# Turning q and k on VectorE in 32x32 blocks, from the seventh head pair on

## The chip, the core and the metric

The kernel runs on one core of a Trainium2 chip. A core has five engines that run their own instruction streams in order and wait for one another through semaphores: PE (TensorE, the matrix unit; its weight loads are listed apart as PEld), DVE (VectorE), ACT (ScalarE), POOL (GpSimd) and SP (SyncE, which here only issues DMAs). SBUF is the working memory of 128 partitions; PSUM, in eight banks, is where PE writes.

The metric is the device time of one execution in microseconds (us). Before the change the median of three runs is 283.14 us (282.72 to 283.64).

## The reference, cut to what matters

Inputs are q, k, v of shape (batch 4, heads 8, tokens 768, dim 64) in fp32. Each token of q and of k gets a 6-bit bucket: the signs of its six products with the columns of `proj`. A query attends only to the keys of its own bucket:

```
q_bits = einsum(q, proj) > 0          # 6 signs for each token
k_bits = einsum(k, proj) > 0
mask   = bucket(q)[:, None] == bucket(k)[None, :]
attn   = softmax(where(mask, q @ k.T / 8, -1e9))
x      = (attn @ v), heads joined to (4, 768, 512)
x_prev = x shifted by one token
xk, xr = mu * x + (1 - mu) * x_prev    # two mixes
out    = sigmoid(xr @ w_r) * (relu(xk @ w_k) ** 2 @ w_v)
```

## The kernel before

**Pairs and slots.** The eight heads of a batch are handled as four pairs, so there are 16 pairs `n`, and `NPB` is 4. A pair has 12 slots: two heads `j`, each with six chunks `jc` of 128 keys. In a slot, `score` (L319) makes a 128x768 tile of scores on PE with two matmuls, and ACT takes its exponential into `pt` (L332). Two slots later `pv` (L340) multiplies six blocks of `pt` with v and adds them up in a PSUM bank `oo`; after the sixth chunk DVE divides by the sum (L363, L364) into `ob`.

**The mask inside the score.** The operands of the score have 70 rows: 64 of the head's turned q or k, and 6 of plus or minus one half for the bucket bits (tiles `aq`, `ak`, three sets used in turn). Equal buckets give a product larger by enough that after the scaled exponential all other keys vanish.

**Preparing a pair.** This is the part that the change touches. `load_qk` (L227) brings q and k of a pair in with tokens on partitions: partition p holds the six tokens 6p to 6p+5. `turn` (L263) transposes three 128x128 fp32 blocks of one head of one side on PE (L269) into a PSUM bank; DVE copies them to `tq` (L272) or scales them to `tk` (L274); then POOL casts one half to bf16 into `aq` or `ak` (L277) and DVE the other (L278). There are four such calls for each pair. `bits` (L281) multiplies the turned tiles with `proj` (L287), DVE makes plus or minus one half of the signs (`sg`, L291), and eight small DMAs on the SP queue put them under the operands (L297). `norm` (L254) adds up squares on ACT for a check of the range at the end; a pair below `NKEEP` = 6 has its norms only in the tail of the kernel. `values` (L302) casts v on POOL and sums it.

**The second half: mixing and the channel mix.** `turn_out` (L371) transposes `ob` on PE (L378), DVE copies it to `xt` (L379), and POOL (DVE for the last pair of a batch) makes the copy shifted by one token (L384). `mix` (L389) is three steps on DVE: a difference `df` (L394), times mu (L398), plus the shifted tile (L405). The matmuls of the channel mix (L424) are a list of items with costs in us of PE (`ffn_items`, L508), first `k` and `r` items and then `v` items; `ffn` (L524) plays them out twice in each slot, so that the channel mix of one batch fills the slots of the next batch. Results of `k` items go through a relu on ACT (L447) or DVE (L449) and a square on DVE (L455), of `r` items through a tanh on ACT (L464), of `v` items through DVE (L487) to the output DMA (L491).

**What sets the order.** The schedule is written by hand: the loop from L605 on issues everything slot by slot, and each engine runs its own instructions in that order. With s for the slot in pair n: loads of pair n+3 and of v at s = 3 (5 in the first pair); `bits` for n+1 at s = 1 (3 in the first); `turn_out` of n-1 at s = 3; the first mix at s = 4, the second at s = 8; the four turns for n+2 at s = 5, 7, 9, 11; `values` at s = 6 and 10; `norm` for n+1 at s = 8 and 10, from n+1 = 6 on. `later` (L214) postpones an instruction by a number of slots. PSUM banks go by letter: two score tiles, and single banks A to D. From pair 4 on, the outputs of both heads use bank A, turns, bits and `turn_out` use B, and the channel mix C and D. The weights w_v come through two staging tiles (`load_wv`, L542) and are cast by POOL (L550) eight slots after their load is issued.

## Time and profile before

The profiled execution took 281.45 us; its span, from the first to the last instruction, is 279.6 us. It lies 1.69 us below the median of the timed runs.

| | before |
|---|---|
| median of 3 runs | 283.14 us |
| profiled execution, and its span | 281.45 us, 279.6 us |
| PE busy | 262.2 us (94%) |
| ACT busy | 215.0 us (77%) |
| DVE busy | 198.6 us (71%) |
| POOL busy | 113.3 us (41%) |
| DMA moved | 29.95 MB, mean 107 GB/s |
| pairs 0 to 3, without the channel mix | up to about 58.7 us |
| pairs 4 to 15, with it | about 58.7 to 243.5 us |
| channel mix of the last batch alone | about 243.5 us to the end |

In a timeline, a line begins with the start and the duration in us, then the engine, the line of the kernel, the operation, output and inputs with their shapes, and in brackets how long the engine sat idle before it and what ended the wait. The duration of a matmul includes the time that it spends in the pipe beside its neighbours; what it costs in a row of matmuls is the distance from one start to the next.

### The profile page before, as it was taken

To read this page: it belongs to the slowest core of one execution; us is meant where nothing else is said; L and a number is where in the kernel's file an instruction comes from. 1 tells how busy PE (TensorE), PEld (TensorE's weight loads), DVE (VectorE), ACT (ScalarE), POOL (GpSimd) and SP (SyncE) were. 2 spreads that over 40 slices of the span, in tenths; PEclk is the share of its full clock that TensorE was granted. 3 is DMA by queue.
4 is the path that set the end of the run, shared out by engine and by line. 5 is a ranking of instruction groups with operands and counts; after the bars stand their busy time and mean duration, and the time that the engine had idled before them with its cause. 6 is when DMAs were issued, how large, how long until landed. Compare 5 with 4: busy or idle time off the path is not lost.

```text
span 279.6 us, 6894 instructions
## 1 busy us (share of the span) xinstructions
PE 262.2 (94%) x2530; PEld 165.4 (59%) x2561; DVE 198.6 (71%) x438; ACT 215.0 (77%) x318; POOL 113.3 (41%) x300
## 2 busy tenths in 40 slices
PE   7999997899999999999999999999999889989991
PEld 5466765666565665656565765656565556545540
DVE  3766839879997866769698766769698835576541
ACT  2199995898799896878989896878998898449800
POOL 5885667665554350714455260715444600000000
PEclk9999997999999999999999999999999999999997
DMA  7459597253213050726122040815220001320042
GB/s 231 167 115 208 179 328 248 43 173 101 77 59 117 6 172 4 218 110 191 59 69 108 14 164 7 272 53 166 84 60 4 5 2 39 114 76 2 0 151 86
DMA packets 19896, 29.95 MB, mean 107 GB/s; under 512 B 2184, under 2 KB 15056, under 8 KB 19856
## 3 DMA queue, kind: packets, MB, share of 16 engines
q1 hardware_dynamic: 17928, 25.89, 27.9%
q0 software_dynamic: 1536, 3.15, 5.3%
q8 instruction: 22, 0.36, 0.5%
q10 hardware_dynamic: 392, 0.40, 0.5%
q14 instruction: 18, 0.15, 0.2%
HBM read 24.12 MB, written 6.29 MB: 109 GB/s over the span
## 4 chain that ended last, share of the span: by engine, by line
PE 66%; ACT 9%; DVE 8%; DMA 7%; issue 3%; SPq 3%; POOL 2%; ACTq 0%; DVEq 0%
PE sc L325 15%; PE vp L424 13%; PE kp L424 12%; PE oo L352 8%; ACT pt L332 6%; PE rp L424 5%; DMA wvs<-in_moe_w_v_dram 4%; PE bb L287 4%; PE tpq L269 3%; PE tpk L269 2%; SPq L297 2%; PE ot L378 2%; ACT sq L256 2%; PE oo L343 1%; DMA aq<-sg 1%
## 5 line engine op out<-in xcount | busy, mean ns | idle before, releaser
L332 ACT ACTIVATE pt<-sc,expb 128x768 bf16<-128x768 f32 x192 | 166.5, 904 | 39.4 <-PE sc L325 38.1
L325 PE MATMUL sc<-aq,ak 70*128 70x384 bf16 x384 | 94.9, 328 | 3.2 <-ACT pt L332 0.8
L352 PEld LDWEIGHTS <-pt 128*128 128x128 bf16 x1152 | 61.1, 98 | 26.6 <-issue 0.8
L352 PE MATMUL oo<-va,pt 128*128 128x65 bf16 x1152 | 66.9, 194 | 0.0
L424 PE MATMUL kp<-xk,wk_sb 128*128 128x384 bf16 x256 | 57.7, 325 | 0.8 <-DVE os L487 0.8
L325 PEld LDWEIGHTS <-ak 70*128 70x128 bf16 x384 | 34.9, 98 | 29.3 <-issue 9.1
L424 PE MATMUL vp<-wv_sb,k 128*128 128x512 bf16 (+1 forms) x186 | 50.3, 370 | 0.4 <-issue 0.2
L277 POOL CAST aq<-tq 64x384 bf16<-64x384 f32 x32 | 21.1, 658 | 63.3 <-DVE tq L272 63.3
L455 DVE TENSOR_TENSOR k<-kr 128x384 bf16<-128x384 bf16 x64 | 29.0, 459 | 15.5 <-ACT kr L447 14.3
L424 PEld LDWEIGHTS <-wk_sb 128*128 128x128 bf16 x256 | 22.2, 97 | 13.3 <-issue 4.2
L256 ACT ACTIVATE sq<-qk 128x768 bf16<-128x768 f32 x32 | 27.1, 847 | 0.1
L424 PE MATMUL rp<-wr_sb,xr 128*128 128x512 bf16 x79 | 24.9, 379 | 1.2 <-DVE kr L449 0.8
L424 PEld LDWEIGHTS <-k 128*128 128x128 bf16 x200 | 17.5, 97 | 12.0 <-issue 2.7
L447 ACT ACTIVATE kr<-kp 128x384 bf16<-128x384 f32 x36 | 17.7, 491 | 7.4 <-PE kp L424 7.4
L487 DVE SCALAR_TENSOR_TENSOR os<-th,vp 128x512 f32<-128x512 bf16 (+1 forms) x25 | 16.5, 663 | 9.0 <-PE vp L424 8.9
L384 POOL COPY xt<-xt 128x127 bf16<-128x127 bf16 x12 | 3.6, 302 | 46.4 <-DVE xt L379 46.4
L311 POOL TENSOR_TENSOR s<-vf 128x192 f32<-128x192 f32 x32 | 20.8, 650 | 0.0
L277 POOL CAST ak<-tk 64x384 bf16<-64x384 f32 x32 | 19.3, 602 | 2.4 <-DVE tk L274 2.4
L274 DVE TENSOR_SCALAR tk<-tpk 128x384 f32<-128x384 f32 x32 | 17.6, 550 | 3.4 <-PE tpk L269 3.3
L272 DVE COPY tq<-tpq 128x384 f32<-128x384 f32 x32 | 17.7, 552 | 2.1 <-PE tpq L269 2.0
L269 PE MATMUL tpq<-ident,qk 128*128 128x128 f32 x96 | 16.9, 287 | 2.4 <-DVE tq L272 1.7
L379 DVE COPY xt<-ot 128x768 bf16<-128x768 bf16 x16 | 8.9, 558 | 14.3 <-PE ot L378 14.2
(60 smaller groups left out, 320.0 us busy)
## 6 DMA issues: line engine op xcount, KB each, us to landing
vf<-in_v_dram SPq DMA_DIRECT2D x16, 384.0 KB
out_dram<-os SPq DMA_DIRECT2D x23, 256.0 KB
qk<-in_q_dram SPq DMA_DIRECT2D x13, 384.0 KB
qk<-in_k_dram SPq DMA_DIRECT2D x13, 384.0 KB
wvs<-in_moe_w_v_dram SPq DMA_DIRECT2D x4, 512.0 KB
aq<-sg SPq DMA_DIRECT2D x64, 4.5 KB
wk_sb<-in_moe_w_k_dram POOLq DMA_DIRECT2D x2, 512.0 KB, 5.4
ak<-sg SPq DMA_DIRECT2D x62, 4.5 KB
```

The source lines that it names most:

```text
L256: nc.scalar.activation(junk, nats[n][:, i].rearrange("p j f -> p (j f)"), AF.Square, accum_out=nrm[:, i, n : n + 1],)
L269: nc.tensor.transpose(tp[:, cols], nats[n][:, i, j, cols], ident32)
L272: nc.vector.tensor_copy(dst, tp)
L274: nc.vector.tensor_scalar(out=dst, in0=tp, scalar1=ALPHA, scalar2=None, op0=ALU.mult)
L277: nc.gpsimd.tensor_copy(au[side, j][0:D, 0:HALF], dst[0:D, :])
L311: nc.gpsimd.tensor_add(s3, vf[:, 0 : 3 * D], vf[:, 3 * D : 6 * D])
L325: nc.tensor.matmul(sc[:, sp, 0:HALF], au["k", j][:, jc * P : (jc + 1) * P], au["q", j][:, sp * HALF : (sp + 1) * HALF], start=True, stop=True,
L332: nc.scalar.activation(pt.rearrange("p (s q) -> p s q", s=2), sc[:, :, 0:HALF], AF.Exp, bias=expb, scale=SCALE,)
L352: nc.tensor.matmul(oo[:, ic, :], pts[n, j, jc][:, ic * P : (ic + 1) * P], vas[n, j][:, jc, :], start=False, stop=(jc == NC_ - 1 and ic == ...
L424: nc.tensor.matmul(box["t"], lhs(), rhs(), start=(i == 0), stop=(i == len(mms) - 1))
L447: nc.scalar.activation(kr, kp, AF.Relu)
L455: 1, lambda: nc.vector.tensor_tensor(out=k2, in0=kr, in1=kr, op=ALU.mult)
```

## The change

It has four parts.

1. Pairs 6 to 15 are no longer turned on PE. `load_blocks` brings q and k in block rows: for each side and head two DMAs of 32 partitions, one for each half of the 64 dims, with 24 consecutive tokens on a partition. A DMA reads its 6016 bytes of a row in one piece, so the other half of the dims is read along and not used. `turn_blocks` transposes 32x32 blocks on DVE, one instruction for a side of a pair, with both heads in one 128x768 tile; POOL casts the first head to bf16 and DVE the second, one slot later. `bits_blocks` does the projection on these tiles. For these pairs `norm`, `values` and `turn_out` take the matching token order. The loads of pair 5's v and of all from pair 6 on are issued at s = 6 instead of 3; the turns are at s = 6 and 9; `norm` runs one pair earlier.
2. From pair 4 on the second head's output goes to bank B instead of A; `bits` moves from s = 1 to s = 4, `turn_out` from s = 3 to s = 2, and the second mix from s = 8 to s = 7.
3. In pairs 1 to 3 the three steps of the first mix are issued at s = 6, 8 and 10 instead of all at s = 4.
4. The staging of w_v uses the two new block tiles, each for two loads, so that no load waits for a cast, and the cast comes ten slots after the load instead of eight.

```diff
+            blkp = pool("blk", 2)
+            turnp = pool("turn", 1)
-            t32p = pool("t32", 1)
-            stg = pool("stg", 2)
...
+            def load_blocks(n):
+                b, t = divmod(n, NPB)
+                xb = blkp.tile([P, 2, NTOK, D], FP32, name=f"blk{n}", tag="blk")
+                blks[n] = xb
+                run = NTOK * D - 32
+                for side, i, src in SIDES:
+                    for j in range(2):
+                        rows = src[b, 2 * t + j].rearrange("(i u) d -> i (u d)", u=NTOK)
+                        for h in range(2):
+                            r0 = 32 * (2 * j + h)
+                            nc.sync.dma_start(
+                                out=xb[r0 : r0 + 32, i].rearrange("p u d -> p (u d)")[:, 0:run],
+                                in_=rows[:, 32 * h : 32 * h + run],
+                            )
...
+            def turn_blocks(n, i):
+                side = "qk"[i]
+                au = augs[n % NSET]
+                tt = turnp.tile([P, S], FP32, name=f"t{side}{n}", tag=f"t{side}")
+                nc.vector.transpose(
+                    out=tt.rearrange("p (c i u) -> p u c i", c=NC_, u=4),
+                    in_=blks[n][:, i, :, 0:32].rearrange("p (u c) d -> p u c d", u=4),
+                )
+                turned[n, side] = tt
+
+                def cast(eng, j):
+                    src = tt[j * D : (j + 1) * D, :]
+                    dst = au[side, j][0:D, :]
+                    if side == "q":
+                        eng.tensor_copy(dst, src)
+                    else:
+                        eng.tensor_scalar(
+                            out=dst, in0=src, scalar1=ALPHA, scalar2=1.0,
+                            op0=ALU.mult, op1=ALU.mult,
+                        )
+
+                cast(nc.gpsimd, 0)
+                later(1, lambda: cast(nc.vector, 1))
...
-            def mix(b, dc, i):
+            def mix(b, dc, i, steps=(0, 1, 2)):
...
             def load_wv(c0):
-                st = stg.tile([P, 2, DM], FP32, name=f"wvs{c0}", tag="stg")
+                if c0 in (0, 4):
+                    mx["wvs"] = blkp.tile([P, 2, 2, DM], FP32, name=f"wvs{c0}", tag="blk")
+                st = mx["wvs"][:, c0 % 4 // 2]
...
-                    8,
+                    10,
...
-                return "AC"[j] if n < NPB else "A"
+                return "AC"[j] if n < NPB else "AB"[j]
...
-                if live and s == (5 if n == 0 else 3):
+                if live and s == (5 if n == 0 else 3 if n < NPB - 1 else 6):
                     if n + 3 < NPAIRS:
-                        load_qk(n + 3)
+                        (load_qk if n + 3 < NKEEP else load_blocks)(n + 3)
...
-                    if s == (3 if n == 0 else 1) and n + 1 < NPAIRS:
-                        bits(n + 1, (0, 1), mb)
-                    if s == 3 and n >= 1:
+                    if s == (3 if n == 0 else 1 if n < NPB else 4) and n + 1 < NPAIRS:
+                        if n + 1 < NKEEP:
+                            bits(n + 1, (0, 1), mb)
+                        else:
+                            bits_blocks(n + 1, mb)
+                    if s == (3 if n < NPB else 2) and n >= 1:
                         turn_out(n - 1, mb)
-                    if s == 4 and n >= 1:
+                    if s == 4 and n >= NPB:
                         mix((n - 1) // NPB, (n - 1) % NPB, 0)
+                    if s in (6, 8, 10) and 1 <= n < NPB:
+                        mix(0, n - 1, 0, [s // 2 - 3])
...
-                    if n > NPB and s == 8:
+                    if n > NPB and s == 7:
                         mix((n - 1) // NPB, (n - 1) % NPB, 1)
-                    if s in (5, 7, 9, 11) and n + 2 < NPAIRS:
+                    if s in (5, 7, 9, 11) and n + 2 < NKEEP:
                         x = (s - 5) // 2
                         turn(n + 2, x % 2, x // 2, mb)
+                    if s in (6, 9) and NKEEP <= n + 2 < NPAIRS:
+                        turn_blocks(n + 2, s // 9)
...
-                    if s in (8, 10) and NKEEP <= n + 1 < NPAIRS:
-                        norm(n + 1, (s - 8) // 2)
+                    if s in (8, 10) and NKEEP <= n + 2 < NPAIRS:
+                        norm(n + 2, (s - 8) // 2)
```

## The prediction

> **What bounds the kernel now.** I read the page first, then the busy time by pair, then the timelines of single engines inside one pair.
>
> ```profile
> span 279.6 us, 6894 instructions
> PE 262.2 (94%) x2530; PEld 165.4 (59%) x2561; DVE 198.6 (71%) x438; ACT 215.0 (77%) x318; POOL 113.3 (41%) x300
> PE   7999997899999999999999999999999889989991
> ACT  2199995898799896878989896878998898449800
> ```
>
> PE is the busiest engine in every slice, but ACT shows eights and nines beside it for most of the span. The average does not say which of the two would stop a faster PE, so I cut the span from one pair's bits to the next:
>
> ```profile
> core 0: us, PE busy (x) PEld busy (x) DVE busy (x) ACT busy (x) POOL busy (x), PEclk, DMA share, GB/s
> 58.72:73.11 14.39, 13.56 (x152) 9.05 (x149) 12.74 (x30) 13.10 (x20) 8.08 (x21) 1.00 0.47 165
> 104.64:120.05 15.41, 15.25 (x153) 9.48 (x155) 10.93 (x24) 12.17 (x17) 6.23 (x17) 1.00 0.41 133
> 135.93:151.63 15.70, 15.51 (x158) 10.00 (x160) 13.81 (x31) 14.30 (x23) 6.59 (x17) 1.00 0.23 80
> 198.13:213.80 15.67, 15.36 (x161) 9.83 (x167) 13.82 (x30) 14.58 (x24) 6.87 (x20) 1.00 0.10 30
> 213.80:228.76 14.96, 13.29 (x135) 7.81 (x138) 9.21 (x21) 13.00 (x21) 4.31 (x14) 1.00 0.02 4
> ```
>
> The rows are pairs 4, 7, 9, 13 and 14. A full pair takes 15.2 to 15.9 us, and PE is busy for all but 0.2 to 0.3 us of it. There are two kinds. Where the channel mix plays `v` items (pair 7), ACT needs 12.2 us and DVE 10.9: PE alone is the bound. Where it plays `k` and `r` items (pairs 9, 13), ACT is at 14.3 to 14.6 us and DVE at 13.8: three engines are nearly full. Pair 14 has no turns already and still takes 14.96 us with PE busy 13.29.
>
> **1. Turns leave PE (pairs 4 to 13 issue them).** The cost of a turn is read from the starts in pair 7:
>
> ```profile
> 111.78 0.49 PE L325 MATMUL sc<-aq,ak 70*128 70x384 bf16 x2
> 112.10 0.35 PE L352 MATMUL oo<-va,pt 128*128 128x65 bf16 x6
> 112.50 0.49 PE L269 MATMUL tpk<-ident,qk 128*128 128x128 f32 x3
> 112.83 0.38 PE L424 MATMUL vp<-wv_sb,k 128*128 128x512 bf16 x1
> ```
>
> Three transposes hold PE from 112.50 to 112.83, 0.33 us. Four calls a pair make 1.3 us, ten pairs 13 us; that is the most this part can give. The bits stay at four matmuls (0.78 us a pair) and only move. How much of the 1.3 us arrives depends on ACT:
> - Pairs 7, 8, 11, 12 (ACT 12.2 to 12.7 us in the same table): PE stays the bound at 14.1 us and ACT would be 86 to 90% full. I take 1.2 us each, 4.8 us.
> - Pairs 6, 9, 10, 13 (ACT 14.8, 14.3, 14.3, 14.6): PE would need about 14.4 us, as much as ACT. Two engines that wait for each other through two score tiles do not both run full; today ACT reaches 91 to 93% here. At 95% the pairs take 15.6, 15.1, 15.1 and 15.3 us: gains 0.3, 0.6, 0.7, 0.35, together 1.95 us.
> - Pair 5 (15.59 us, ACT 13.3): 0.9 us.
> - Pair 4: its first half has no channel mix, and it now gets two norms (0.83 us each between starts) that pair 5 had; the last two leave pair 14. ACT goes from 13.1 to 14.8 us, more than the pair lasts today: a loss of 0.5 us. Pair 14 loses 1.66 us of ACT work; of its 1.7 us of PE gaps I take back 0.7 us.
>
> Sum: 4.8 + 1.95 + 0.9 - 0.5 + 0.7 = 7.85 us.
>
> **2. What DVE gets instead.** For one pair it loses these (mean ns after the bar):
>
> ```profile
> L272 DVE COPY tq<-tpq 128x384 f32<-128x384 f32 x32 | 17.7, 552 | 2.1 <-PE tpq L269 2.0
> L274 DVE TENSOR_SCALAR tk<-tpk 128x384 f32<-128x384 f32 x32 | 17.6, 550 | 3.4 <-PE tpk L269 3.3
> L278 DVE CAST ak<-tk 64x384 bf16<-64x384 f32 x32 | 15.3, 479 | 1.1
> L278 DVE CAST aq<-tq 64x384 bf16<-64x384 f32 x32 | 12.1, 377 | 1.1
> L277 POOL CAST aq<-tq 64x384 bf16<-64x384 f32 x32 | 21.1, 658 | 63.3 <-DVE tq L272 63.3
> ```
>
> 4 x 0.55 + 2 x 0.48 + 2 x 0.38 = 3.9 us. It gets two 128x768 fp32 turns, which no row shows. Low end: the slope between the 384-element copy (0.55) and the 512-element L487 (0.68) is about 1.05 ns an element, so 0.95 us. High end: each of the 24 blocks pays one smallest DVE instruction (the 0.059 us memset) on top: 2.4 us. The nearest row is the fp32 copy, so I take 1.0 us. The two casts double in size: from 0.38 us, at most 0.75 each. New sum 2 x 1.0 + 2 x 0.75 = 3.5 us, 0.4 less; with 2.4 us a turn it is 6.3 us, 2.4 more. This lies beside PE and ACT and costs nothing while DVE stays under them: 13.8 - 0.4 = 13.4 us of about 15.1 in pair 9. Its cover is gone at the high end (16.2 us), which is a rival below.
>
> [...]
>
> POOL gets two casts of 768 elements (0.8 to 1.0 us by the 128x1024 cast, 1.03 us) for four of 0.6 to 0.66: no change on an engine 6 to 8 us busy a pair. But the order turns round: today DVE and POOL are released together and DVE's cast starts at once; now POOL starts first and DVE comes a slot later. A DVE cast beside a busy POOL took 3.06 us at 46.85, against 0.35 alone. So a cast can be held by 0 to 2.7 us, and the squares and copies behind it on DVE too. POOL's runs around the casts are 1 to 3 us; I expect 0.5 us each, inside DVE's room.
>
> **3. Loads and the SP queue.** Two q and k loads (0.38 to 0.47 us of SP each) become eight, and the bytes double, by about 0.75 MB a pair. An SP issue costs 0.38 us at the least (output) and 0.7 us (bits), so eight cost 3.0 to 5.6 us instead of 0.9. With bits 5.6, v 0.4 and at most four outputs 1.6, SP is busy 10.6 to 13.2 us of 14.2. The bytes add about 0.16 to a DMA share of 0.23 to 0.47 (147 GB/s at 0.45). Blocks are needed 12 slots after their issue, bits 8 slots, some 9 us, against about 5 us of issue and landing. I cost it at nothing; the cover is these slots, and beyond them PE waits for bits or DVE for a block.
>
> **4. Bank B, `turn_out` at s = 2, bits at s = 4, mix at s = 7.** The wait of head 1's first `pv` for bank A was 0.2 us in all, so the bank gives 0 to 0.2 us. The earlier `turn_out` leaves one slot less for the division: PE has 1.14 us of work between the last `pv` and the transposes (three half-slots of channel mix, 0.27 each, and a score, 0.33), and at the end of pair 7 DVE finished `ob` 1.0 us after that `pv` (119.74 to 120.73). With DVE late PE waits: 0 to 0.6 us a pair; 0.1 in eleven pairs is 1.0 us lost. POOL's shifted copy gets a slot more, so DVE's waits of 0.4 us for it go; they are not on the path.
>
> **5. The early stretch.** Here a wait is on the path (lines of four engines):
>
> ```profile
> 36.78 1.04 POOL L550 TENSOR_SCALAR wv_sb<-wvs 128x1024 bf16<-128x1024 f32 x1 [1.79 <-DMA wvs<-in_moe_w_v_dram]
> ...
> 41.23 0.56 DVE L394 TENSOR_TENSOR df<-xt 128x768 bf16<-128x768 bf16 x1 [3.52 <-POOL xt L384]
> ...
> 43.36 0.55 PE L269 MATMUL tpq<-ident,qk 128*128 128x128 f32 x3 [1.75 <-DVE tq L272]
> ...
> 44.33 1.87 ACT L332 ACTIVATE pt<-sc,expb 128x768 bf16<-128x768 f32 x2 [1.86 <-PE sc L325]
> ```
>
> POOL stands on a w_v load, the shifted copy is late, DVE waits 3.52 us in the mix with a turn's copy behind it, then PE and ACT, the bound in pairs 0 to 3, wait. ACT's gaps from 43 to 52 us add up to 3.8 us. With the cast two slots later and the mix two slots behind the copy, this chain should go. Late next are the 0.4 us gaps at each set of bits. Ends 0 and 3.3 us; I take 2.0, since a second cast still meets POOL's descriptor work for w_r.
>
> **Sum.** 7.85 + 2.0 - 1.0 = 8.85 us from 281.45 us is 272.6 us. Since that execution is 1.69 us below the median of the runs, I forecast 274.3 us for the median after.
>
> **Rivals.**
> - *ACT takes the whole place of PE in the `k` pairs.* The 1.95 us goes, pairs 4 and 5 give nothing, the early chain is halved: 4.8 - 0.5 + 0.7 + 1.0 - 1.0 = 5.0 us, 278 us. For it: ACT 14.3 to 14.8 us. Against: PE and ACT idle at different moments today.
> - *All of it arrives.* 13 + 3.3 = 16.3 us, 267 us. Against: pair 14 with no turns needed 14.96 us.
> - *DVE becomes the bound; slower.* If a turn costs 2.4 us and the POOL order holds both casts 1 us each, DVE in pairs 4, 5, 6, 9, 10, 13 needs about 13.4 + 2.8 + 2 = 18.2 us against 15.7: 15 us lost in six pairs, 6.8 won elsewhere: 291 us. It decides from about 16 us of DVE work a pair. Against: the fp32 copies run at 1.05 ns an element, and pair 7 has 4.5 us of DVE to spare.
>
> That the turns don't leave PE is excluded: PE's stream has no L269 block for pairs 6 to 15.
>
> **Chances and range.** Forecast (270 to 277): 0.52. ACT (277 to 282): 0.18. All of it (266 to 270): 0.10. DVE bound or held, above 284: 0.17. Nothing measurable (within 0.3%, what a measurement of this kernel can tell from no change): 0.03. 8 in 10 lie between 268 and 285. Faster 0.79, same 0.04, slower 0.17.
>
> **What the profile after would show.** Right: no PE transposes of q or k after 60 us, pairs 7, 8, 11, 12 at 14.1 to 14.4 us with PE full, pairs 9, 10 near 15 us with ACT above 94%, no DVE wait of 3.5 us for the shifted copy near 41 us, the new turn at about 1 us. Wrong: turns near 2 us or DVE casts held for a microsecond, PE waiting for DVE in `k` pairs, or scores waiting for bits because SP is late. What makes it wrong first is the unseen turn and the order of the two casts.

## The result, and the profile after

The changed kernel takes 293.65 us (median of 4 runs, 292.53 to 294.64), against 283.08 us (282.72 to 283.64) for the kernel before beside it: ratio 1.037, 95% interval 1.0335 to 1.0402. It is 10.6 us slower. The forecast was 274.3 us, with 268 to 285 as its range; the rival that came nearest is the slower one, at 291 us. The profiled execution took 292.92 us, its span is 291.1 us.

Below, each experiment is told by its difference to the kernel before run on the same chip, whose median was 282.0 to 282.5 us there. In three experiments some executions ran at a lower granted clock than the rest (0.954 against 0.970 to 0.982 in one of 4 with the old slots, 0.978 against 0.984 to 0.995 in one of 10 with three places moved, 0.974 to 0.980 against 0.984 to 0.994 in 4 of 10 with the signs' place alone); the ratios leave those out, so a ratio need not be the quotient of the two medians.

The first lines of the page of the kernel after, and its slices of PE and ACT:

```profile
span 291.1 us, 6646 instructions
...
PE 254.1 (87%) x2412; PEld 151.2 (52%) x2441; DVE 211.4 (73%) x398; ACT 215.9 (74%) x318; POOL 111.2 (38%) x280
...
PE   7899999988696989997896979997896999989990
...
ACT  2298887979587797968789777877888888539800
```

PE lost 8.1 us of busy time and 7 points of share; from the eleventh slice on it has slices of six and seven, where before every slice from the eighth to the last but one was eight or nine. No engine is busier than 87%. DVE rose from 198.6 to 211.4 us although it was forecast to fall a little. The busy time by pair, cut from one pair's output transposes to the next; the rows are pairs 7, 9 and 14:

```profile
core 0: us, PE busy (x) PEld busy (x) DVE busy (x) ACT busy (x) POOL busy (x), PEclk, DMA share, GB/s
110.76:125.71 14.95, 14.29 (x141) 7.95 (x142) 11.83 (x20) 12.31 (x17) 6.35 (x17) 1.00 0.58 148
...
143.31:161.22 17.91, 14.73 (x145) 8.64 (x149) 15.15 (x26) 13.57 (x21) 6.12 (x16) 1.00 0.51 120
...
226.36:241.18 14.82, 13.84 (x144) 8.26 (x146) 8.43 (x20) 12.88 (x19) 4.01 (x14) 1.00 0.02 5
```

Pair 7, which plays `v` items, gained 0.5 us; pair 14, with ACT relieved of the norms, 0.3. Pair 9, which plays `k` items, went from about 15.7 to 17.9 us, with PE busy 14.7, ACT 13.6 and DVE 15.2: none is full. What stands between them is shown by DVE's timeline in pair 9, from the sign's threshold on (start, duration, in brackets the idle time before it and what ended it):

```profile
147.18 0.56 DVE L353 TENSOR_SCALAR sg<-bb 128x384 bf16<-128x384 f32 x1 [2.33 <-PE bb L345]
...
150.03 1.57 DVE L319 STREAM_TRANSPOSE tq<-blk 128x768 f32<-128x768 f32 x1
...
151.82 1.66 DVE L329 CAST aq<-tq 64x768 bf16<-64x768 f32 x1
...
155.53 1.59 DVE L319 STREAM_TRANSPOSE tk<-blk 128x768 f32<-128x768 f32 x1
...
157.33 1.62 DVE L331 TENSOR_SCALAR ak<-tk 64x768 bf16<-64x768 f32 x1
...
159.53 0.55 DVE L539 TENSOR_SCALAR kr<-kp 128x384 bf16<-128x384 f32 x1
```

DVE stands idle for 2.33 us on the sign matmuls `bb`, which the change moved to slot 4, and then works without a gap from 147.18 to past 161 us: mix, turn, cast, division, mix, turn, cast. The relu `kr` that PE needs to get its PSUM bank back stands at the end of that row; PE waited 1.27 us for it, until 160.13. Three things show in it: a wait that was not there, a turn of 1.57 us where 1.0 was costed, and casts of 1.6 us. The groups (count, busy us and mean ns after the bar):

```profile
L319 DVE STREAM_TRANSPOSE tk<-blk 128x768 f32<-128x768 f32 x10 | 15.7, 1566 | 0.0
L319 DVE STREAM_TRANSPOSE tq<-blk 128x768 f32<-128x768 f32 x10 | 15.6, 1560 | 0.0
L329 DVE CAST aq<-tq 64x768 bf16<-64x768 f32 x10 | 10.9, 1089 | 0.3
L331 DVE TENSOR_SCALAR ak<-tk 64x768 bf16<-64x768 f32 x10 | 9.6, 961 | 0.3
L545 DVE TENSOR_TENSOR k<-kr 128x384 bf16<-128x384 bf16 x64 | 25.9, 413 | 11.7 <-ACT kr L537 10.9
```

And the waits in pairs 4 to 14 (us in total, times, longest):

```profile
ACT pt L419 <- PE sc L412: 28.9, 38, 3.4
DVE sg L353 <- PE bb L345: 19.6, 10, 2.7
PEld L464 <- DVE ob L451: 9.2, 10, 2.8
PE kp L514 <- DVE kr L539: 9.0, 7, 1.9
PE ot L464 <- DVE ob L451: 5.5, 6, 2.4
PE rp L514 <- DVE kr L539: 3.2, 3, 2.0
```

In the kernel before the same two waits, in pairs 4 to 14, were:

```profile
DVE sg L291 <- PE bb L287: 0.7, 3, 0.2
PE rp L424 <- DVE kr L449: 0.8, 1, 0.8
```

Now PE waits 12.2 us for relus and 5.5 us for the division `ob`, both DVE's, and ACT waits for PE's scores.

### The profile page after: what moved, and what is told of

Same layout as the page of the kernel before. It is cut to its first block, busy times and chain, and to the rows that moved or that the text cites. A ratio compares the mean times of both kernels' runs of the same rounds, so it can differ in the third digit from the quotient of the medians.

```text
span 291.1 us, 6646 instructions
## 1 busy us (share of the span) xinstructions
PE 254.1 (87%) x2412; PEld 151.2 (52%) x2441; DVE 211.4 (73%) x398; ACT 215.9 (74%) x318; POOL 111.2 (38%) x280
## 2 busy tenths in 40 slices
DMA packets 18296, 37.48 MB, mean 129 GB/s; under 512 B 3144, under 2 KB 10896, under 8 KB 18256
## 4 chain that ended last, share of the span: by engine, by line
PE 40%; DVE 34%; DMA 11%; ACT 5%; issue 4%; SPq 3%; POOL 1%; ACTq 0%; DVEq 0%
PE vp L514 9%; PE sc L412 8%; PE kp L514 7%; PE oo L439 4%; PE rp L514 4%; DMA vf<-in_v_dram 4%; DVE tq L319 4%; DVE tk L319 3%; ACT pt L419 3%; DVE aq L329 3%; DVE ob L451 3%; DVE k L545 3%; DMA qk<-in_k_dram 2%; PE bb L345 2%; DVE xk L496 2%
## 5 line engine op out<-in xcount | busy, mean ns | idle before, releaser
L419 ACT ACTIVATE pt<-sc,expb 128x768 bf16<-128x768 f32 x192 | 166.7, 905 | 46.2 <-PE sc L412 44.1
L412 PEld LDWEIGHTS <-ak 70*128 70x128 bf16 x384 | 34.9, 98 | 36.4 <-issue 15.1
L329 POOL CAST aq<-tq 64x768 bf16<-64x768 f32 x10 | 9.8, 980 | 66.7 <-DVE tq L319 53.3
L545 DVE TENSOR_TENSOR k<-kr 128x384 bf16<-128x384 bf16 x64 | 25.9, 413 | 11.7 <-ACT kr L537 10.9
L537 ACT ACTIVATE kr<-kp 128x384 bf16<-128x384 f32 x36 | 17.9, 496 | 9.4 <-PE kp L514 9.4
L514 PEld LDWEIGHTS <-k 128*128 128x128 bf16 x200 | 16.7, 97 | 13.6 <-issue 3.7
L398 POOL TENSOR_TENSOR s<-vf 128x192 f32<-128x192 f32 x32 | 22.5, 704 | 0.0
L353 DVE TENSOR_SCALAR sg<-bb 128x384 bf16<-128x384 f32 x10 | 5.6, 558 | 19.6 <-PE bb L345 19.6
L331 POOL TENSOR_SCALAR ak<-tk 64x768 bf16<-64x768 f32 x10 | 10.4, 1042 | 22.0 <-DVE tk L319 22.0
L451 DVE TENSOR_TENSOR ob<-oo,rc 128x384 bf16<-128x384 f32 x32 | 17.8, 558 | 1.1
L539 DVE TENSOR_SCALAR kr<-kp 128x384 bf16<-128x384 f32 x28 | 15.4, 550 | 2.6 <-PE kp L514 2.5
L287 ACT ACTIVATE sq<-blk 128x768 bf16<-128x768 f32 x20 | 17.0, 849 | 0.0
L319 DVE STREAM_TRANSPOSE tk<-blk 128x768 f32<-128x768 f32 x10 | 15.7, 1566 | 0.0
L319 DVE STREAM_TRANSPOSE tq<-blk 128x768 f32<-128x768 f32 x10 | 15.6, 1560 | 0.0
```

The source lines that it names most:

```text
L287: nc.scalar.activation(junk.rearrange("p (u d) -> p u d", u=NTOK), blks[n][:, i, :, 0:32], AF.Square, scale=1.5, accum_out=nrm[:, i, n : n ...
L319: nc.vector.transpose(out=tt.rearrange("p (c i u) -> p u c i", c=NC_, u=4), in_=blks[n][:, i, :, 0:32].rearrange("p (u c) d -> p u c d", u=4),
L329: eng.tensor_copy(dst, src)
L398: nc.gpsimd.tensor_add(s3, vf[:, 0 : 3 * D], vf[:, 3 * D : 6 * D])
L412: nc.tensor.matmul(sc[:, sp, 0:HALF], au["k", j][:, jc * P : (jc + 1) * P], au["q", j][:, sp * HALF : (sp + 1) * HALF], start=True, stop=True,
L419: nc.scalar.activation(pt.rearrange("p (s q) -> p s q", s=2), sc[:, :, 0:HALF], AF.Exp, bias=expb, scale=SCALE,)
```

## The experiments

The rows below are the times in us from one pair's first output transpose to the next, read from PE's timeline of each profiled execution. A kernel that issues the output transposes at slot 2 shows the last slot in pair 15, so its sum is about 1.5 us longer for that alone.

```
pair                         4     5     6     7     8     9    10    11    12    13    14    15   sum
before                    15.6  15.5  15.8  15.5  16.0  15.6  15.7  15.5  15.3  15.5  15.1  11.2  182.3
after                     17.1  19.3  15.8  14.9  17.6  17.9  16.7  14.9  17.0  16.5  14.8  12.7  195.3
dense turn                16.7  15.9  15.4  14.3  16.7  16.7  16.1  14.4  16.4  15.3  14.8  12.7  185.5
places alone on before    16.2  16.8  16.5  15.8  17.2  16.6  16.6  15.8  16.3  15.6  15.9  12.7  192.0
signs earlier, as written 16.0  16.7  15.0  14.2  16.6  16.3  14.6  14.2  15.8  18.2  13.9  11.2  182.7
signs earlier, dense turn 15.6  15.5  14.6  14.2  15.5  15.4  14.2  14.2  14.7  15.4  14.0  11.2  174.5
the same, squares out     14.8  14.8  14.6  14.2  15.2  15.6  14.2  14.2  14.7  14.6  14.0  11.2  172.1
```

### The turn itself: how it is written, and whether it is there

The theory after the result had three parts: the turn is longer than costed because it writes every fourth word; DVE's cast is held by POOL; and the new slots bunch DVE's work behind one wait. The rivals were ScalarE as the second bound and the doubled loads.

The turn written into consecutive words:

```diff
-                    out=tt.rearrange("p (c i u) -> p u c i", c=NC_, u=4),
+                    out=tt.rearrange("p (u c i) -> p u c i", c=NC_, u=4),
```

> The DVE turn writes each block as 32 neighbouring words instead of every fourth word (the tokens land in another order, so this leaves out the right order of the output). If the step of four words is what makes a turn 1.56 us, it falls to 0.95 us. Theory A: 12 us less DVE in twenty turns, seven tenths of them in k pairs: 5 to 8 us faster than the changed kernel, 286 to 289. B and C: no change. If the turn stays at 1.56 us, the step is not the reason for its length, and no theory expects a change.

Measured: 282.94 us, 0.9 us above before, ratio 1.002 (0.9987 to 1.0054), so 9.6 us less than the changed kernel when each is set against its own runs of before. The turn falls to 0.97 us.

The same write order with blocks loaded to suit it, so that the tokens come out in order:

```diff
-run = NTOK * D - 32
+run = NC_ * D - 32
-rows = src[b, 2 * t + j].rearrange("(i u) d -> i (u d)", u=NTOK)
+rows = src[b, 2 * t + j].rearrange("(u i c) d -> i u (c d)", u=4, c=NC_)
...
-                    out=tt.rearrange("p (c i u) -> p u c i", c=NC_, u=4),
+                    out=tt.rearrange("p (c u i) -> p u c i", c=NC_, u=4),
```

> The changed kernel with another order of tokens in the block rows: each partition gets four runs of six tokens, 192 tokens apart, so that the DVE turn writes 32 neighbouring words and the tokens still land in order; nothing is left out. Theory A (the four-word step of the turn's writes, 12 us of DVE in the chain of the k pairs, is the loss): a turn takes 0.97 us as in the run with dense writes and the time is 280 to 285 us, about that before the change. Theory C (form and bytes of the loads): shorter runs of 1408 bytes in four times as many packets make it slower than the dense run, above 286 us.

Measured: 282.31 us, 0.2 below before, ratio 0.999 (0.9958 to 1.0024): the same time as before, and 10.7 us less than the changed kernel. The turns in its groups:

```profile
L321 DVE STREAM_TRANSPOSE tq<-blk 128x768 f32<-128x768 f32 x10 | 9.7, 971 | 0.0
L321 DVE STREAM_TRANSPOSE tk<-blk 128x768 f32<-128x768 f32 x10 | 9.7, 966 | 0.0
```

20 turns are 11.9 us shorter, and the time is 10.7 us shorter: between these two lengths the turn is on the path nearly one to one. (In the table 3.4 of the 9.8 us lie in pair 5, where the changed kernel's profile has stretches of halved TensorE clock, 0.50 granted; the last section comes to them.) This kernel moves 25,976 DMA packets against 18,296 of the changed kernel, whose loads the run before it has too. It is not slower than that run for it (282.31 against 282.94 us), so the number of packets is not what costs; the doubled bytes are in both.

The turn left out altogether:

```diff
-                tt = turnp.tile([P, S], FP32, name=f"t{side}{n}", tag=f"t{side}")
-                nc.vector.transpose(...)
+                tt = turned[NKEEP - 1, side]
```

> The DVE turn is left out for pairs 6 to 15: their operands are cast from the last turned tile of pair 5 (the outputs of these pairs are not computed). 31 us less DVE work, PE's stream the same. Theory A: the chain in k pairs falls from 13 to 10 us, below PE's 14 us: 271 to 278 us, under the time before the change. B: PE still waits for ob and DVE for bits: 290 us or more. C: no change, 293.

Measured: 279.96 us, 2.0 below before, ratio 0.990 (0.9833 to 0.9956). That missed the expectation: DVE's busy time falls from 211.4 to 183.1 us, and the pairs with `k` items, 14.9 to 15.9 us from pair 8 on, are hardly shorter than before. Against the dense turn another 19.4 us of turns are gone, and the time is only about 2 us shorter: that far the nearly one to one does not reach. DVE still waits 14.5 us for `bb` here. So with the change's slots something else holds those pairs. (Its profiled execution also has a stretch of halved TensorE clock near 60 us, 0.50 granted; the last section comes to that.)

### The casts

DVE's cast issued first and POOL's behind it:

```diff
-                cast(nc.gpsimd, 0)
-                later(1, lambda: cast(nc.vector, 1))
+                cast(nc.vector, 1)
+                cast(nc.gpsimd, 0)
```

> DVE's bf16 cast is issued right behind its turn and ahead of POOL's, instead of a slot later and behind it. Theory A (in the pairs with k items DVE is one unbroken chain from bits to the next pair's turn_out, and PE waits for its end): the held casts fall from 1.09 and 0.96 us to about 0.56 each, 9 us less DVE in twenty casts, of which the eleven or twelve in k pairs are on the chain: 4 to 6 us faster than the changed kernel, 287 to 290 us. Theory B (the new slots of bits and turn_out make PE wait, DVE's work is hidden): no change, 293 to 294. Theory C (the doubled bytes and the later loads hold the pairs): no change.

Measured: 292.40 us, 10.4 above before, ratio 1.0365 (1.0325 to 1.0405): nothing gained that can be told. The groups say why:

```profile
L545 DVE TENSOR_TENSOR k<-kr 128x384 bf16<-128x384 bf16 x64 | 33.6, 535 | 11.9 <-ACT kr L537 11.0
L331 DVE TENSOR_SCALAR ak<-tk 64x768 bf16<-64x768 f32 x10 | 5.6, 555 | 0.3
L329 DVE CAST aq<-tq 64x768 bf16<-64x768 f32 x10 | 5.6, 555 | 0.3
```

The casts fall by 9.3 us in all, as expected, and the squares behind them rise by 7.7 us (mean 413 to 535 ns). The time that the casts lost beside POOL did not go away; most of it came back on the squares. In the changed kernel's own trace the longest row of squares, two in 1.52 us at 224.09, lies beside POOL's cast `ak` (223.09 to 224.28) and its work on v; with POOL idle, from 226.25 on, one takes 0.36 us.

### The places

The slots of the kernel before, and bank A for both heads, put back into the changed kernel:

```diff
-                return "AC"[j] if n < NPB else "AB"[j]
+                return "AC"[j] if n < NPB else "A"
-                    if s == (3 if n == 0 else 1 if n < NPB else 4) and n + 1 < NPAIRS:
+                    if s == (3 if n == 0 else 1) and n + 1 < NPAIRS:
-                    if s == (3 if n < NPB else 2) and n >= 1:
+                    if s == 3 and n >= 1:
-                    if n > NPB and s == 7:
+                    if n > NPB and s == 8:
```

> Part 2 of the change is undone: bits at s = 1, turn_out at s = 3, second mix at s = 8, both heads in bank A; turns stay on DVE. Theory A: DVE's work is the same, but no longer starts behind bits at s = 4 where DVE sat idle 2 us a pair; 2 to 6 us faster than the changed kernel, 288 to 291, still slower than before the change. B: the waits for ob (14 us) and for bits (20 us of idle DVE) go: 270 to 276 us. C: no change.

Measured: 291.84 us, by the ratio 9.0 above before, ratio 1.032 (1.0252 to 1.0386). The wait for the signs went, and others came in its place (waits of this kernel in pairs 4 to 15):

```profile
PE oo L430 <- POOL s L399: 11.8, 5, 2.6
...
PE oo L430 <- DVE ob L451: 4.5, 4, 2.3
...
DVE sg L353 <- PE bb L345: 1.0, 4, 0.2
```

`oo` is a head's output, which must wait for bank A until DVE has divided the head before it. In five rows POOL's sum `s` is written as what ended the wait. But the matmul reads `vs`, which had been written 7.9 to 12.1 us before, and in each of these rows a division `ob` ended 0.14 to 0.15 us before the matmul began, as it did in the row of 2.30 us at 135.62 us that names it. So it is the division, DVE's, that PE waits for here too. By itself this run could not clear the places, since it changed the bank too; it does show that the wait for the signs goes with their slot, since they were in bank B here as well.

The slots alone on the kernel before (bank A kept, turns on PE kept):

```diff
-                    if s == (3 if n == 0 else 1) and n + 1 < NPAIRS:
+                    if s == (3 if n == 0 else 1 if n < NPB else 4) and n + 1 < NPAIRS:
-                    if s == 3 and n >= 1:
+                    if s == (3 if n < NPB else 2) and n >= 1:
-                    if n > NPB and s == 8:
+                    if n > NPB and s == 7:
```

> The kernel before, turns on PE, with only the slots of part 2: bits at s = 4, turn_out at s = 2, second mix at s = 7 (both heads stay in bank A). If the slots themselves cost time because DVE stands idle for bits and PE for ob: 2 to 5 us slower than before, 284 to 287 us. If they are neutral (theory A): within 1 us of before.

Measured: 290.46 us, 8.0 above before, ratio 1.028 (1.0251 to 1.0314), more than any theory gave. There is no VectorE turn in this kernel and no load in block rows, and yet the waits for the signs and for the division are there as in the changed kernel (PE's wait for relus is small, 1.7 us):

```profile
DVE sg L291 <- PE bb L287: 19.5, 10, 2.7
PEld L378 <- DVE ob L364: 6.1, 10, 2.0
PE ot L378 <- DVE ob L364: 3.1, 4, 1.7
```

### The early parts alone, and ScalarE

Parts 3 and 4 of the change on the kernel before (its own two staging tiles kept, the cast of w_v ten slots after its load):

```diff
-                    8,
+                    10,
...
-                    if s == 4 and n >= 1:
+                    if s == 4 and n >= NPB:
+                    if s in (6, 8, 10) and 1 <= n < NPB:
+                        mix(0, n - 1, 0, [s // 2 - 3])
```

> The kernel before with part 3 and the cast of w_v ten slots after its load (two staging tiles as before). My term of 2.0 us for the early stretch: 280 to 281.5 us, the fourth pair's turn_out 1.5 to 2 us earlier. Rival: the gain is given back in pair 4, 282 us.

Measured: 280.29 us, 2.2 below before, ratio 0.993 (0.9899 to 0.9958). The third row of output transposes starts at 48.6 us instead of 50.7, the fourth, in pair 4, at 58.8 instead of 60.7, and the pairs from 4 on are as before. The wait of 3.52 us is gone in the changed kernel as well; its `df` there has no idle time before it:

```profile
41.04 0.75 DVE L482 TENSOR_TENSOR df<-xt 128x768 bf16<-128x768 bf16 x1
```

ScalarE relieved of the squares for the norms, on the kernel with the dense turn:

```diff
-                    if s in (8, 10) and NKEEP <= n + 2 < NPAIRS:
+                    if s in (8, 10) and NPAIRS <= n + 2 < NPAIRS:
```

> The kernel with the dense turn and its order of tokens, without the squares on ACT for pairs 6 to 15 (the range check sees zeros for them): 1.66 us less ACT in each of pairs 4 to 13. If ACT stops PE in the k pairs once the turns have left it (the first rival of the prediction): 5 to 9 us faster than the same kernel with norms, 273 to 278. If DVE's chain stops it: within 2 us of it.

Measured: 280.36 us, 2.1 below before, ratio 0.9925 (0.9895 to 0.9955), 1.9 below the dense turn with the norms. 17 us of ACT's squares gave 2: with these places ACT was not what stopped PE in the main. Pair 6 gained 1.2 us, pairs 4 and 8 0.7 each, pairs 9 and 13 nothing. Its profiled execution has a stretch of halved clock (0.50) in pair 5, which took 18.7 us instead of 15.9, so the 2 us may be low; the later pairs have none.

### The signs earlier

If the wait for `bb` is the cause, the sign matmuls must go where PE reaches them early and no bank is in the way. Bank A is free from about slot 8 to the end of slot 2, since the second head now uses bank B. With the dense turn:

```diff
-                    if s == (3 if n == 0 else 1 if n < NPB else 4) and n + 1 < NPAIRS:
+                    if s == (3 if n == 0 else 1 if n < NPB else 0) and n + 1 < NPAIRS:
-                            bits(n + 1, (0, 1), mb)
+                            bits(n + 1, (0, 1), mb if n < NPB else "A")
...
-                            bits_blocks(n + 1, mb)
+                            bits_blocks(n + 1, "A")
-                    if s == (3 if n < NPB else 2) and n >= 1:
+                    if s == 3 and n >= 1:
-                    if n > NPB and s == 7:
+                    if n > NPB and s == 8:
```

> The kernel with the dense turn and its matching loads, with three places changed from pair 6 on: the sign matmuls of the next pair go to slot 0 in bank A, which is free from slot 8 to the end of slot 2, instead of slot 4 in bank B; the output's transposes go back to slot 3 and the mix for receptance to slot 8. Theory S (the change's places put VectorE's work of a pair behind one wait for the sign matmuls of slot 4, 18.8 us of idle VectorE in ten pairs, and cost 8.2 us on the kernel before): that idle time falls below 6 us, pairs with k projections come to 14.8-15.6 us, and the time to 275-279 us. Theory D (VectorE's work itself, about 13 us a pair with the held casts, sets the pairs however it is placed): the pairs with k projections stay at 16-16.7 us and the time at 281-284 us.

Measured: 273.58 us, 8.7 below before, ratio 0.971 (0.9653 to 0.9771). It beats both kernels, and lies just under the range that theory S gave. Its waits, and its pairs 7, 9 and 14:

```profile
DVE sg L355 <- PE bb L347: 5.3, 5, 1.2
...
PE kp L516 <- DVE kr L541: 3.0, 4, 0.8
```

```profile
core 0: us, PE busy (x) PEld busy (x) DVE busy (x) ACT busy (x) POOL busy (x), PEclk, DMA share, GB/s
105.71:119.88 14.17, 14.01 (x140) 8.12 (x142) 10.75 (x19) 12.11 (x17) 6.27 (x15) 1.00 0.74 178
...
135.35:150.76 15.41, 14.37 (x148) 8.80 (x150) 13.20 (x24) 14.38 (x23) 6.08 (x16) 1.00 0.54 122
...
209.29:223.24 13.95, 13.10 (x137) 8.26 (x138) 8.07 (x17) 12.49 (x18) 4.30 (x14) 1.00 0.02 4
```

Pair 7 is full of PE again, at 14.17 us: the turn's 1.3 us arrived there whole. Pair 14 gained 1.1 us. Pair 9 stays near the time of before, 15.4 us. PE's wait for the division at the output transposes is no longer in the list.

The changed kernel as it is, turn and loads included, with the same three places:

```diff
-                    if s == (3 if n == 0 else 1 if n < NPB else 4) and n + 1 < NPAIRS:
+                    if s == (3 if n == 0 else 1 if n < NPB else 0) and n + 1 < NPAIRS:
-                            bits(n + 1, (0, 1), mb)
+                            bits(n + 1, (0, 1), mb if n < NPB else "A")
...
-                            bits_blocks(n + 1, mb)
+                            bits_blocks(n + 1, "A")
-                    if s == (3 if n < NPB else 2) and n >= 1:
+                    if s == 3 and n >= 1:
-                    if n > NPB and s == 7:
+                    if n > NPB and s == 8:
```

> The changed kernel itself, with its loads and its turn written every fourth word, and only the three places of the earlier-signs run. Theory S alone (places are the larger part): 280-285 us, since VectorE then has room for part of the longer turn (1.56 against 0.97 us, 11.9 us in twenty turns). Theory D (VectorE's total work decides, places do not): 288-293 us. The difference to the dense run with the same places says what the longer turn costs when VectorE does not wait for slot 4: 10-12 us if VectorE is full, 0-4 us if it has room.

Measured: 281.18 us, 1.1 below before, ratio 0.996 (0.9921 to 1.0001). Three issue places move the changed kernel by 11.7 us. The longer turn costs 7.6 us here by the medians, 7.0 by the ratios, between the two answers that were written down: DVE has room for some four tenths of it.

Of the three places only the signs' moved:

```diff
-                    if s == (3 if n == 0 else 1 if n < NPB else 4) and n + 1 < NPAIRS:
+                    if s == (3 if n == 0 else 1 if n < NPB else 0) and n + 1 < NPAIRS:
-                            bits(n + 1, (0, 1), mb)
+                            bits(n + 1, (0, 1), mb if n < NPB else "A")
...
-                            bits_blocks(n + 1, mb)
+                            bits_blocks(n + 1, "A")
```

> The changed kernel with one place moved: the sign matmuls of the next pair go to slot 0 in bank A; the output's transposes stay at slot 2 and the mix for receptance at slot 7. Theory S1 (the wait of VectorE for the sign matmuls of slot 4 is the whole cost of the places): 280-283 us, as with all three places moved (281.2). Theory S2 (the output's transposes one slot earlier, where TensorE waits for the output's normalisation, and the mix one slot earlier carry a part): 284-289 us. If the sign matmuls' slot is not the cause: 291-294 us, as the changed kernel.

Measured: median 283.63 us, ratio 0.997 (0.9924 to 1.0012), within the interval of the run with all three moved. In the changed kernel the place of the signs (slot and bank, moved together) is the whole of the places' cost as far as these runs can tell; the output transposes at slot 2 still wait for `ob` (6.4 us of weight loads in its list), and what that costs lies within the two intervals, a microsecond or two at the most.

All four casts on DVE, with the signs earlier and the dense turn:

```diff
-                cast(nc.gpsimd, 0)
+                cast(nc.vector, 0)
                 later(1, lambda: cast(nc.vector, 1))
```

> As the run with the sign matmuls in slot 0, but all four casts of a pair are VectorE's, so that GpSimd casts nothing there. Theory H (the cast that GpSimd runs holds VectorE's two-input instructions or its cast, and this is what VectorE lacks): four casts of 0.56 us take the place of two of 1.0-1.1 us, the squares of the k units fall from a mean above 0.40 us to 0.36 us, and the time is 1-3 us below the run before. Theory N (VectorE has room once the places are right): within 1 us of it.

Measured: 277.30 us, 5.0 below before, ratio 0.982 (0.9797 to 0.9849): 3.7 us more than with POOL's half of the casts. Both theories missed. DVE's busy time rises from 201.9 to 204.3 us: its casts take 22.6 instead of 20.0, the squares fall by 3.6 us (to a mean of 0.38, nearly as written down), and the mix's difference `df`, which now runs beside POOL's work on v, rises from 9.8 to 11.9. In the profiles 2.6 us of the loss lie in pair 12 (17.35 instead of 14.74 us), where PE waited 1.8 us for a relu and a stretch of halved clock (0.50) followed, and 1.3 us in pair 10. How much each of these causes costs was not separated.

### What holds the pairs with k items

Even with the good places these pairs are no shorter than with the transposes on PE. The squares of the units whose relu is DVE's, left out:

```diff
-                        nc.vector.tensor_scalar(out=kr, in0=kp, scalar1=0.0, scalar2=None, op0=ALU.max)
+                        nc.vector.tensor_scalar(out=k2, in0=kp, scalar1=0.0, scalar2=None, op0=ALU.max)
+                        return
...
```

> The dense turn with the signs earlier (273.6 us), and the squares of those k units left out whose relu VectorE computes (28 of 64, some 0.4 us each, about four in each pair with k projections): those units go on unsquared. Theory D (VectorE's work, 13.2-13.9 of 15.4 us, sets the pairs with k projections now that TensorE's transposes are gone): these pairs come down from 15.4 to 14.2-14.7 us and the time to 266-270 us. Rival P (TensorE or ScalarE sets them): 15.0-15.4 us, and 272-274 us.

Measured: 271.02 us, ratio 0.960 (0.9548 to 0.9647), 2.6 below the run with them, between the two answers that were written down. In the table pairs 4, 5 and 13 came down by 0.7 to 0.8 us, as theory D has it; pairs 8 and 9 did not (15.2 and 15.6). In pair 9 ACT is at 14.4 of 15.6 us, and two of the squares that remain take 1.39 and 1.32 us, beside POOL's casts from 137.92 to 139.19 and from 143.32 to 144.97, while the next, at 148.72, takes 0.36:

```profile
138.01 1.39 DVE L547 TENSOR_TENSOR k<-kr 128x384 bf16<-128x384 bf16 x1 [0.23 <-ACT kr L545]
...
143.85 1.32 DVE L547 TENSOR_TENSOR k<-kr 128x384 bf16<-128x384 bf16 x1
```

The same squares left out of the kernel before:

```diff
-                        nc.vector.tensor_scalar(out=kr, in0=kp, scalar1=0.0, scalar2=None, op0=ALU.max)
+                        nc.vector.tensor_scalar(out=k2, in0=kp, scalar1=0.0, scalar2=None, op0=ALU.max)
+                        return
...
```

> The kernel before with the same 28 squares left out. Theory D: TensorE sets its pairs with k projections (15.1-15.8 of 15.5-16.0 us), so the time stays within 1.5 us of before, 281-283 us. If VectorE's work set them before as well: 275-279 us.

Measured: 281.76 us, 0.7 below before, ratio 0.9975 (0.9948 to 1.0001), as theory D has it: DVE did not set the pace before. So where the turns have left PE, DVE's work sets part of the time of pairs 4, 5 and 13; what keeps pairs 8 and 9 at 15.2 to 15.6 us, DVE's held squares or ACT, is not settled.

## Why the prediction was wrong, step by step

Two steps failed: the turn was costed at 1.0 us and took 1.56 (step 2), and the bits at slot 4 were costed at nothing (step 4). Both lengthen DVE's row of work and waits, which step 2 held to cost nothing.

**Step 1, the turns leave PE: right in sum once two other terms are taken away, in part by luck.** The forecast was 7.85 us from pairs 4 to 15. With the dense turn and the signs earlier these pairs take 174.5 us instead of 182.3: 7.8 us. It does not fall where the step put it. Gained were 1.2, 1.3, 0.5 us in pairs 6 to 8, 0.2 in 9, 1.5 and 1.3 in 10 and 11, 0.5 and 0.1 in 12 and 13, 1.1 in 14, and nothing in 4 and 5, where the step had a loss of 0.5 and a gain of 0.9. (Its windows began two slots earlier, at the bits, so single pairs compare loosely.) Pairs 8 and 12 gave less than the 1.2 us forecast, and pairs 10 and 14 more than was costed; that these cancel is luck. Pairs 7 and 11, with PE alone as bound, gave 1.3 us where 1.2 was forecast; where `k` items play through the whole pair, there was little. And the reason given for these pairs, ACT, was not it under the change's places: without 17 us of norms pairs 9 and 13 stayed. With the better places ACT is at 14.4 of 15.4 us in pair 9, and whether it stops PE there was not tested.

**Step 2, the turn: the first term that was mis-sized.** It took 1.0 us a turn by the fp32 copy, between 0.95 and 2.4. Measured: 1.56 us as the change writes it, 0.97 us with consecutive words. The nearest row was right for an instruction that writes in rows, and this one doesn't: 1.56 us over 768 elements is 2.0 ns an element, 0.97 us is 1.3. But the right length alone would not have mended the forecast, since the step priced DVE's time only where DVE's sum exceeded the pair: by its own sum two turns of 1.56 us instead of 1.0 bring DVE in pair 9 from 13.4 to about 14.5 us, by my estimate, still under the 15.1 that the step gave the pair. Here twelve microseconds more of DVE's time cost 10.7 us with the change's places and 7.0 to 7.6 with the better ones. In the changed kernel's pairs with `k` items throughout, DVE's busy time is 14 to 15 us of 16.5 to 18 (19.3 in pair 5, with a halved clock).

That is the real fault of step 2: "costs nothing while DVE stays under" the other engines. DVE works through its row in order, has one long wait in it and is waited for at the end of it, and so it sets the pair at its work plus its wait. In pair 9 this is 15.15 us of work and 2.33 us of wait, 17.5 of 17.9 us. The casts that ran beside POOL's cost what the step had, 0.4 to 0.55 us each in the mean (0.96 and 1.09 us against 0.56 in the run with DVE's cast first), but not "inside DVE's room", since in these pairs there was none.

**Step 3, loads and the SP queue: right in the time.** More packets cost nothing (25,976 against 18,296: 282.31 against 282.94 us), and in the changed kernel's list of waits for pairs 4 to 14 no row names a DMA. The share of the DMA engines rose by more than the 0.16 that the step had, in pair 9 from 0.23 to 0.51, and no engine waited for it.

**Step 4, the places: the second term that failed.** The step costed the bank and the earlier output transposes, 1.0 us, and gave nothing to the bits at slot 4. The places alone cost 8.0 us on the kernel before and 11.7 us on the changed one, and there the signs' place is all of it but a microsecond or two. On the kernel before the three places were not moved one by one, so what share of the 8.0 us is the signs' stays open. The step saw what the move does for PE and the SP queue and did not ask what stands behind `sg` on DVE: the mix, both turns, the division and the relus.

**Step 5, the early stretch: right by itself, but little of it is left in the changed kernels.** 2.0 us were forecast and 2.2 measured on the kernel before (the interval allows 1.2 to 2.9). With the dense turn and the signs earlier, pair 4's output transposes start at 60.00 us instead of 60.70, so only 0.7 us is left there: the sign matmuls before them take 1.9 us (56.02 to 57.94), in which PE waits for DVE's `tk`, instead of 0.8 on the kernel with the early parts alone.

The sum, against the kernel before beside it: +10.6 us measured, 8.85 us less forecast, 19.4 us apart. Dense turn and earlier signs together take 19.3 us away (from +10.6 to -8.7), so the miss is these two. That the 8.7 us come so near to the forecast 8.85 is luck in part, since the early stretch gave less there and the output transposes, back at slot 3, cost nothing. One by one they take 10.7 and 11.7 us, 3.1 us more than together, as would be if each also gives DVE room that hides part of the other; that was not tested by itself.

**The rivals.** *DVE becomes the bound* had the sign and almost the time, 291 us, by other numbers: it wanted turns of 2.4 us and casts held a full microsecond, and "about 16 us of DVE work a pair". It happened at 14 to 15 us of work with turns of 1.56 us, because of the wait. So its nearness to 293.65 us is luck, and its chance, 0.17, was too small because the wait was not in it. *ACT takes the whole place of PE* is against the run without norms, as far as the change's places go. *All of it arrives* needs 1.3 us from every pair, and pairs 4 and 5 gave none even in the best version.

**The signs to look for.** The prediction named "turns near 2 us or DVE casts held for a microsecond, PE waiting for DVE in `k` pairs" as what would show it wrong. The last two are in the fences above: casts of 1.62 and 1.66 us in pair 9, and PE's waits for `kr` and `ob`. The turn of 1.57 us lies halfway between the 1.0 that was costed and that sign.

## What to carry to other kernels

Before work is moved to an engine, write down its instructions in their order with the waits between them, and ask who waits for the last one: work plus wait is what to compare with the pair, not busy time. When an issue place is moved, list what is queued behind the consumer of its result on the consumer's engine; here the place of one group of matmuls cost more than the whole change was to win. Price an unseen instruction by its access pattern as well as by its size, and try the pattern with consecutive writes first: the same 128x768 turn took 1.56 us here with every fourth word written and 0.97 us with consecutive ones.

## What the chip showed that I had not expected

**Behind a short gap of PE its clock was halved for 3.4 us, in some cases.** The changed kernel, in pairs 4 to 6 of its profile (the figure after the busy times is the granted clock):

```profile
75.00:77.00 2.00, 1.32 (x9) 0.98 (x10) 1.93 (x5) 0.00 (x0) 0.00 (x0) 0.57 0.92 217
77.00:79.00 2.00, 2.00 (x18) 1.30 (x17) 0.36 (x2) 0.84 (x2) 0.35 (x1) 0.58 0.08 20
91.00:93.00 2.00, 1.64 (x14) 1.07 (x14) 1.43 (x3) 1.29 (x3) 1.92 (x5) 0.84 1.06 238
93.00:95.00 2.00, 2.00 (x8) 0.88 (x7) 1.11 (x4) 1.01 (x2) 0.43 (x4) 0.50 1.00 214
95.00:97.00 2.00, 1.95 (x24) 1.54 (x24) 1.19 (x3) 0.54 (x2) 0.35 (x1) 0.81 0.85 216
```

Each stretch follows a wait of PE:

```profile
75.68 0.82 PE L464 MATMUL ot<-ident,ob 128*128 128x128 bf16 x6 [2.42 <-DVE ob L451]
...
91.36 0.81 PE L514 MATMUL kp<-xk,wk_sb 128*128 128x384 bf16 x4 [1.88 <-DVE kr L539]
```

Summed over the five rows, two microseconds times what the clock lacks, 3.4 us of clock are lost; if all of it is on the path, that is near a third of the 11.5 us between the two profiled executions. (The profile of the kernel before has one such stretch too, from about 44.1 to 47.5 us behind a wait of 1.75 us, so the two differ by half of that.) In the other profiles such stretches, 3.4 us long or twice that, came with waits of PE of 1.8 to 2.7 us, and no kernel whose PE never waited over 1.4 us between 58 and 240 us had one there. Not every such wait is followed by one: after waits of 1.95 us (at 172 us in this same profile), 2.03 us (dense turn, at 75 us) and 2.45 us (the old slots in the changed kernel, at 103 us) the clock stayed whole. No run changed such a gap by itself, so what decides between the two outcomes stays open.

**The hold between POOL and DVE moves rather than goes.** A square of 0.36 us took 1.39 us beside casts on POOL; freeing the casts put 7.7 of their 9.3 us onto the squares, and taking the casts off POOL put 2.1 us onto the mix. In the changed kernel it goes with the order of the starts: the nine of DVE's twenty casts that began 0.09 to 0.33 us behind POOL's cast of the same tile took 1.42 to 1.67 us, and the eleven that began 0.05 to 0.11 us ahead of it took 0.55 to 0.56, while POOL's took 1.14 to 1.19 us there instead of 0.82. What the two engines share was not tested.
